# Channel group 1 of a long convolution goes through its products as stationary operand instead of a turn through DRAM, with strided PSUM evictions, q in long rows and a new written order

## The chip, the cores and the metric

The kernel runs on one core of one Trainium2 chip. The metric is device time in microseconds (us): 199.32 us is the median of three timed runs of the kernel before (198.66 to 200.85). A separate execution was recorded by the hardware profiler. The engines are TensorE (PE, matmuls and, beside them, its weight loads, PEld), VectorE (DVE), ScalarE (ACT), GpSimd (POOL) and SyncE (SP), which here issues every DMA. SBUF is the memory that the engines work in, PSUM the small memory that PE writes to and that DVE and ACT empty ("evict").

## The reference

Two independent computations on 2048 positions and 576 channels, in bf16, whose results stand side by side in the output (2048 x 1152).

```python
# A: a gated long convolution
k_shift = sum(k_pad[:, t:t+S, :] * shift_k[:, 3 - t] for t in range(4))   # 4 taps along the positions
kv = k_shift * v
y = causal_convolution(kv, ssm_k)      # length 2048 per channel, by FFT of 4096
y = y + kv * ssm_D
a = q * y
# B: linear attention, 32 heads of 18 channels
q, k, v = split(x @ wqkv)
phi = lambda t: where(t > 0, t + 1, exp(t)) + 1e-6
kv = phi(k)^T v ; z = sum(phi(k))      # per head
o = (phi(q) kv) / (phi(q) z + 1e-6)
b = o @ wo
out = concat([a, b], -1)
```

## The kernel before

**Part A.** A position n is written as 16 a + b, with a on the 128 partitions. The convolution is a product of two transforms of 128 x 16 frequencies.

- `conv_piece`: the four taps on DVE or POOL, per piece of 128 channels (`HP`, the last has 64) and half of b: `tap` (L427, products), `tap+` (L432) and `tapx` (L435, sums), `tapv` (L438, product with v).
- `h_piece` and `s1`: PE transposes the filter (L465), `hD` (L477) adds ssm_D into its first row, and `s1` (L515) does the 128-point transform with the table `Gsb` as stationary operand. Its result is evicted into C (`Ch` of the filter, `Cu` of the signal).
- `s2`: DVE transposes 32x32 blocks (L532, `ct`), PE does the 16-point transform in 32x32 tiles (L541), and the result goes into `su`. For the filter pieces in `HDMA` a transposing DMA (L490, `cq`) and a full-width matmul (`s2q`, L498) take the place of these, with an eviction `s2evq` into `TT`. The evictions are made by the helper `copy`: ACT at L259, DVE at L261.
- `inv`: per block of 64 channels, two DMAs swap neighbouring rows of TT (`X`), two products with su are formed on DVE or POOL (L562, `p0` and `p1`), and the inverse 16-point transform follows.
- Its result has to be turned so that the 128 frequencies lie on partitions. Channel groups (`QG`): 0 and 1 have 256 channels, 2 has 64. For the groups in `DR` PE works in 32x32 tiles (`i1`, L572), the result is evicted into U, written to DRAM (`Vw`, tensor `v_scr`) and read back turned as V (`Vr`). For the others the products are the stationary operand (`i1s`, L591), so that the matmul's result is turned already; it is evicted into V directly (`i1evs`), and `i2` reads V with a stride.
- `inv2`: the 128-point inverse transform with the table `Esb` (`i2`, L627 and L630), the product with q (`i2q`, L637), and the store (`yo`).

**Part B.** `kproj` (L660 matmul, L663 exp, L666 the rest of phi) and `qproj` (L678, L682, L686, L689) need x with channels on partitions. Two of the four x tiles are transposed by PE (L336), two by transposing DMAs (L348, L351). `b_G` (L716) forms x^T phi(k), from which `M` (L826) follows; `dmm` gives the denominators, their reciprocal is spread by `b_bc` (L843) and multiplied in (`pqn`, `pqg`). `b_out` (L877) is the output projection, a row block in two halves of five matmuls, with evictions `oev` into ob and a store `oo`.

**What sets the order.** Every operation is registered with `P.op`. The string `PLAN` lists all of them in one written order with the engine that does each (P, A, D, G for POOL, S for SP); an engine takes its own in that order, and so does SP's DMA queue. `PLACES` gives each buffer its address and PSUM bank. `FILL` puts filler matmuls of no use (L927) ahead of some operations. `PORT` names the DVE and POOL operations that work on SBUF alone: one of POOL's is made to wait for the last of DVE's that stands before it in the order.

Of the kernel before, what the change touches and what calls it, by code (L numbers as in the profile page):

```python
# [26 lines left out]
DR = (0, 1)  # L27
# [191 lines left out]
def kernel(  # L219
# [226 lines left out]
    def h_piece(pc):  # L446
# [27 lines left out]
        def hd(e):  # L474
            d = Drow.t[0:1, c0:c0 + n]
            o = hT.t[0:1, 0, :]
            nc.vector.tensor_tensor(  # L477
# [5 lines left out]
        for g in range(n // PCH):  # L483
            sp = SB("TT", [128, 2, 8, 128, 2])
            TX[c0 // PCH + g] = sp
            if not dt:
# [5 lines left out]
                rd=[C], wr=[cq], name="trq", tx=_dma(524288, 256), bias=(nm, 0.0))  # L492
            for hh in range(2):
                ps = psb(2, "s2ps")

                def mm(e, hh=hh, ps=ps, cq=cq):
# [5 lines left out]
                    e, sp.t[:, 0, 4 * hh:4 * hh + 4].rearrange("p w k t -> p w t k"),  # L502
                    ps.t.rearrange("p b (w t k) -> p (b w) t k", w=2, t=2)),
# [51 lines left out]
    def inv(g, su, bias):  # L555
# [28 lines left out]
        for hh in range(2):  # L584
# [10 lines left out]
            def ev(e, hh=hh, ps=ps):  # L595
                o0 = c0 + 32 * hh
                copy(e, V[vg].t[:, :, o0:o0 + 32].rearrange("p r (q j) -> p q r j", j=4),
                     ps.t.rearrange("p b c -> p (b c)").rearrange("p (q r j) -> p q r j", q=8, j=4))
            P.op(either(1024), ev, rd=[ps], wr=[(V[vg], (g, hh))], name="i1evs", bias=bias)

    def inv2(vg, bias):
        c0, n = QG[vg]
        qb = SB("q%d" % vg, [128, 16, n], side=1)
        load("qA", qb, lambda e: dma(qb.t[:], ap(q, c0, [[16 * D, 128], [D, 16], [1, n]])), 4096 * n, row=2 * n,
             bias=(bias[0], -5.0))
        nb = 512 // n
        if vg in DR:
            dtok = P.buf("vd%d" % vg, [128, 1], space="dram")
            for kh in range(4):
                load("Vw", None, lambda e, kh=kh: dma(  # L610
                    ap(V_d[vg], 32 * n * kh, [[128 * n, 32], [1, 32 * n]]),
                    U[vg].t[32 * kh:32 * kh + 32].rearrange("p k c -> p (k c)")), 2048 * n, rd=[U[vg]],
# [5 lines left out]
        for bg in range(16 // nb):  # L618
            ps = psb(1, "i2ps")

            def mm(e, bg=bg, ps=ps):
                for j in range(nb):
                    b = nb * bg + j
                    for ri in range(2):
                        v_ = V[vg].t[:, 2 * b + ri, :]
                        if vg in DR:
                            nc.tensor.matmul(ps.t[:, 0, n * j:n * j + n], lhsT=Esb.t[:, b, ri, :], rhs=v_,  # L627
                                             start=(ri == 0), stop=(ri == 1))
                            continue
                        nc.tensor.matmul(ps.t[:, 0, n * j:n * j + n], lhsT=Esb.t[:, b, ri, :],  # L630
                                         rhs=bass.AP(tensor=v_.tensor, offset=v_.offset,
                                                     ap=[list(v_.ap[0]), [64, n // 64], [1, 4], [4, 16]]),
                                         start=(ri == 0), stop=(ri == 1))

            def mul(e, bg=bg, ps=ps):
                qs = qb.t[:, nb * bg:nb * bg + nb, :]
# [390 lines left out]
```

## Time and profile before

| | before |
|---|---|
| median of three timed runs | 199.32 us |
| profiled execution, its own time | 196.29 us |
| span, first to last instruction | 194.5 us |
| PE busy | 163.6 us (84%), of which fillers at L927 15.4 us |
| DVE busy | 152.1 us (78%) |
| ACT busy | 123.1 us (63%) |
| POOL busy | 86.1 us (44%) |
| mean granted PE clock | 0.957 |
| moved by DMA | 40.52 MB, 208 GB/s in the mean |

An engine's busy time counts its instructions only, not its waits. Matmuls are pipelined, so a busy PE is not PE at its peak. The page's second part cuts the span into 40 slices, one digit each for the busy tenths. The chain of waits goes back from the last instruction, at each step to what released it; "SPq" in it is SP's queue issuing a DMA, "issue" is time without a visible wait. A group row gives line, engine, operation, what it writes and reads with shapes, the count, then busy us and mean ns of one, then the idle time ahead of the group and what ended it.

### The profile page before, as it was taken

The page shows a single profiled execution, that of the slowest core. Times are in us where ns is not written, and L with a number is a line of the kernel's source. Part 1 is how long each engine was busy: PE and PEld are TensorE (multiplying, and loading weights), DVE is VectorE, ACT ScalarE, POOL GpSimd, SP SyncE. Part 2 cuts the span into 40 slices and gives each one's busy share as a digit, 9 for nine tenths or more (in the row PEclk, how much of TensorE's full clock was granted, in tenths as well). Part 3 has the DMA queues.
Part 4 walks back from the last instruction along what each step waited for, and adds up shares of the span by engine and source line. Part 5 has one row for each costly group of instructions (what it writes and reads, how often), then busy time and mean ns, then how long its engine had stood idle before and what let it go on. Part 6 is the DMA issues. An engine that isn't in the chain of part 4 may idle for free.

```text
span 194.5 us, 4394 instructions
## 1 busy us (share of the span) xinstructions
PE 163.6 (84%) x1803; PEld 113.9 (59%) x1812; DVE 152.1 (78%) x182; ACT 123.1 (63%) x174; POOL 86.1 (44%) x47
## 2 busy tenths in 40 slices
PE   7597889989469999999999877779899947998580
PEld 5296657547347756777777454337356626887360
DVE  0019998998978999999989997799999849544370
ACT  2366857666638875425379999999999925424000
POOL 8002367380480081604189999599650250800000
PEclk9759999999969999999999999999999999999697
DMA  5999999898970346590289996424059699999996
GB/s 136 360 380 259 377 243 201 218 275 275 193 222 0 105 98 135 115 357 21 81 228 266 249 181 205 165 108 166 4 108 278 194 276 318 217 266 272 311 264 207
DMA packets 51264, 40.52 MB, mean 208 GB/s; under 512 B 25323, under 2 KB 48108, under 8 KB 50348
## 3 DMA queue, kind: packets, MB, share of 16 engines
q1 hardware_dynamic: 51244, 40.24, 77.7%
q8 instruction: 14, 0.23, 0.5%
q14 instruction: 6, 0.05, 0.1%
HBM read 21.62 MB, written 8.91 MB: 157 GB/s over the span
## 4 chain that ended last, share of the span: by engine, by line
DVE 28%; DMA 27%; PE 19%; ACT 11%; SPq 7%; issue 5%; DVEq 0%; ACTq 0%
DMA wq<-in_B_wqkv_dram 8%; DMA V<-v_scr 7%; DVE m L427 6%; SPq L251 6%; DMA wk<-in_B_wqkv_dram 4%; ACT TT L259 4%; DMA v<-in_A_v_dram 4%; DMA v_scr<-U 4%; PE ps_all L877 4%; PE ps_all L660 3%; DVE hT L477 3%; PE ps_all L678 3%; DVE ct L532 2%; DVE U L261 2%; DVE pqT L689 2%
## 5 line engine op out<-in xcount | busy, mean ns | idle before, releaser
L562 POOL TENSOR_TENSOR TT<-su,TT 128x2048 bf16<-128x2048 bf16 x8 | 32.4, 4070 | 12.4 <-ACT su L259 9.4
L660 PE MATMUL ps_all<-wk,xT 128*128 128x288 bf16 x160 | 22.9, 286 | 3.8 <-DMA xT<-in_B_x_dram 3.3
L432 POOL TENSOR_TENSOR m<-m 128x2048 bf16<-128x2048 bf16 (+1 forms) x4 | 14.3, 3577 | 22.0 <-DVE m L427 14.9
L515 PEld LDWEIGHTS <-Gsb 128*128 128x128 bf16 x320 | 19.2, 102 | 6.0 <-issue 3.5
L660 PEld LDWEIGHTS <-xT 128*128 128x128 bf16 x160 | 15.2, 98 | 10.1 <-DMA xT<-in_B_x_dram 3.6
L427 DVE TENSOR_TENSOR m<-kb,Wj 128x4096 bf16<-128x4096 bf16 (+1 forms) x10 | 20.6, 2071 | 0.0
L663 ACT ACTIVATE ek<-ps_all,neg 128x288 bf16<-128x288 f32 x32 | 15.8, 500 | 7.6 <-PE ps_all L660 6.6
L716 PE MATMUL ps_all<-pk,x_sb 128*128 128x289 bf16 (+1 forms) x160 | 20.6, 287 | 0.0
L678 PE MATMUL ps_all<-xT,wq 128*128 128x512 bf16 x75 | 19.5, 392 | 1.3 <-DMA wq<-in_B_wqkv_dram 0.9
L877 PE MATMUL ps_all<-M,pqT 128*128 128x288 bf16 x128 | 20.0, 286 | 0.0
L637 DVE TENSOR_TENSOR q<-ps_all,q 128x512 bf16<-128x512 f32 x18 | 11.8, 686 | 10.1 <-PE ps_all L627 7.5
L927 PE MATMUL ps_all<-fz 128*128 128x256 bf16 x87 | 15.4, 303 | 5.0 <-DVE fz L906 1.1
L716 PEld LDWEIGHTS <-x_sb 128*128 128x128 bf16 x160 | 15.3, 98 | 4.2 <-issue 0.2
L686 ACT ACTIVATE eq<-ps_all,neg 128x512 bf16<-128x512 f32 x18 | 12.4, 689 | 7.7 <-PE ps_all L678 6.9
L259 ACT ACTIVATE TT<-ps_all 128x1024 bf16<-128x1024 f32 x13 | 16.6, 1307 | 0.3 <-PE ps_all L541 0.3
L666 DVE SCALAR_TENSOR_TENSOR pk<-ek,ps_all 128x288 bf16<-128x288 bf16 x32 | 13.4, 445 | 3.3 <-ACT ek L663 3.3
L259 ACT ACTIVATE Cu<-ps_all 128x1024 bf16<-128x1024 f32 (+1 forms) x16 | 15.3, 1026 | 0.0
L435 POOL TENSOR_TENSOR m<-m 128x1024 bf16<-128x1024 bf16 x4 | 8.5, 2128 | 15.0 <-DVE m L432 15.0
L259 ACT ACTIVATE su<-ps_all 128x1024 bf16<-128x1024 f32 x12 | 12.0, 1060 | 4.9 <-PE ps_all L541 4.9
L627 PE MATMUL ps_all<-V,Esb 128*128 128x256 bf16 x64 | 9.6, 299 | 6.4 <-DMA V<-v_scr 6.4
L438 POOL TENSOR_TENSOR v<-m,v 128x1024 bf16<-128x1024 bf16 (+1 forms) x6 | 11.9, 1977 | 6.4 <-DVE m L427 6.2
L877 PEld LDWEIGHTS <-pqT 128*128 128x128 bf16 x128 | 12.1, 98 | 4.2 <-issue 1.3
(105 smaller groups left out, 328.1 us busy)
## 6 DMA issues: line engine op xcount, KB each, us to landing
TT<-TT SPq DMA_DIRECT2D x18, 256.0 KB, 3.2
v_scr<-U SPq DMA_DIRECT2D x8, 512.0 KB, 6.4
V<-v_scr SPq DMA_DIRECT2D x8, 512.0 KB, 6.4
x_sb<-in_B_x_dram SPq DMA_DIRECT2D x4, 576.0 KB, 7.7
kb<-in_A_k_dram SPq DMA_DIRECT2D x2, 1152.0 KB, 13.6
v<-in_A_v_dram SPq DMA_DIRECT2D x2, 1152.0 KB, 13.3
out_dram<-ob SPq DMA_DIRECT2D x16, 144.0 KB, 4.3
q<-in_A_q_dram SPq DMA_DIRECT2D x2, 1024.0 KB
```

What stands on the lines that cost most here:

```text
L259: nc.scalar.activation(out=o, in_=i, func=ACTF.Copy)
L427: return nc.vector.tensor_tensor(out=m.t[:], in0=i0, in1=i1, op=ALU.mult)
L432: lambda e: tt(e)(out=m.t[:, 0:2], in0=m.t[:, 0:2], in1=m.t[:, 2:4], op=ALU.add),
L515: nc.tensor.matmul(pf[:, n * j:n * j + n], lhsT=Gsb.t[:, 8 * bg + j, ri, :], rhs=src(8 * bg + j), start=True, stop=True)
L562: P.op({"DVE": _dve(2048, 2), "POOL": _pool(2048)}, lambda e, x=x: tt(e)(out=tx.t[:, x], in0=su.t[:], in1=tx.t[:, x], op=ALU.mult), rd=[su ...
L660: nc.tensor.matmul(ps.t[:, 0, 0:HALF], lhsT=xT.t[:, t, 128 * (r % 4):128 * (r % 4) + 128], rhs=wk.t[:, t, HALF * hh:HALF * hh + HALF], sta ...
L663: P.op(("ACT", _act(HALF) + 0.085), lambda e, hh=hh, ps=ps: nc.scalar.activation(out=eb.t[:, hh], in_=ps.t[:, 0, 0:HALF], func=ACTF.Exp, b ...
L666: P.op(("DVE", _dve(HALF)), lambda e, hh=hh, ps=ps: nc.vector.scalar_tensor_tensor(out=pk.t[:, r, HALF * hh:HALF * hh + HALF], in0=eb.t[:, ...
L678: nc.tensor.matmul(ps.t[:, 0, :], lhsT=wq.t[:, t, 128 * c:128 * c + 128], rhs=xTg[g].t[:, t, :], start=(t == 0), stop=(t == 4))
L716: nc.tensor.matmul(ps.t[:, 0, 0:n], lhsT=x_sb.t[:, r, FT[t]:FT[t] + 128], rhs=pk.t[:, r, HALF * hh:HALF * hh + n], start=(r == 0), stop=(r ...
L877: nc.tensor.matmul(ps.t[:, 0, 0:HALF], lhsT=pqT.t[:, c, 128 * r:128 * r + 128] if c < 4 else pqt.t[:, 128 * (r % 8):128 * (r % 8) + 128], ...
L927: nc.tensor.matmul(b.t[:, 0, 0:256], lhsT=fz.t[:, 0:128], rhs=fz.t[:], start=True, stop=True)
```

## The change

`DR` holds group 0 alone, so group 1 takes the way of group 2. `i1evs` writes V in the natural order of channels and reads PSUM with a stride for it; `i2` then reads V without one, in all groups. `s2evq` reads PSUM with a stride and writes SBUF in one run, where it read in one run and wrote every other element. q is one buffer for all channels, loaded in two DMAs with rows of 9216 bytes instead of three with rows of 512 and 128; the products with q and the stores work on slices of it. `hD` joins `PORT`. The planner's prices of two kinds of DMA (`tx`) are changed. `FILL`, `PLAN` and `PLACES` are new: the order, the choice of DVE, ACT or POOL for operations that several can do, and all addresses. The fillers go from 87 to 31.

```diff
-DR = (0, 1)
+DR = (0,)
...
         def hd(e):
...
-            nc.vector.tensor_tensor(
+            return nc.vector.tensor_tensor(
...
                 P.op(either(1024), lambda e, hh=hh, ps=ps, sp=sp: copy(
-                    e, sp.t[:, 0, 4 * hh:4 * hh + 4].rearrange("p w k t -> p w t k"),
-                    ps.t.rearrange("p b (w t k) -> p (b w) t k", w=2, t=2)),
+                    e, sp.t[:, 0, 4 * hh:4 * hh + 4],
+                    ps.t.rearrange("p b (w t k) -> p (b w) k t", w=2, t=2)),
                     rd=[ps], wr=[(sp, hh)], name="s2evq", bias=(nm, 0.0))
...
             def ev(e, hh=hh, ps=ps):
-                o0 = c0 + 32 * hh
-                copy(e, V[vg].t[:, :, o0:o0 + 32].rearrange("p r (q j) -> p q r j", j=4),
-                     ps.t.rearrange("p b c -> p (b c)").rearrange("p (q r j) -> p q r j", q=8, j=4))
+                copy(e, V[vg].t[:, :, c0:c0 + 64].rearrange("p r (j q) -> p r j q", j=4)[:, :, :, 8 * hh:8 * hh + 8],
+                     ps.t.rearrange("p b c -> p (b c)").rearrange("p (q r j) -> p r j q", q=8, j=4))
             P.op(either(1024), ev, rd=[ps], wr=[(V[vg], (g, hh))], name="i1evs", bias=bias)
+
+    qb = SB("q", [128, 16, D], side=1)
+    for hh in range(2):
+        load("qA", qb, lambda e, hh=hh: dma(qb.t[:, 8 * hh:8 * hh + 8, :], ap(
+            q, 8 * hh * D, [[16 * D, 128], [D, 8], [1, D]])), 1179648, wr=[(qb, hh)], row=9216)
...
-        qb = SB("q%d" % vg, [128, 16, n], side=1)
-        load("qA", qb, lambda e: dma(qb.t[:], ap(q, c0, [[16 * D, 128], [D, 16], [1, n]])), 4096 * n, row=2 * n,
-             bias=(bias[0], -5.0))
...
                     for ri in range(2):
-                        v_ = V[vg].t[:, 2 * b + ri, :]
-                        if vg in DR:
-                            nc.tensor.matmul(ps.t[:, 0, n * j:n * j + n], lhsT=Esb.t[:, b, ri, :], rhs=v_,
-                                             start=(ri == 0), stop=(ri == 1))
-                            continue
                         nc.tensor.matmul(ps.t[:, 0, n * j:n * j + n], lhsT=Esb.t[:, b, ri, :],
-                                         rhs=bass.AP(tensor=v_.tensor, offset=v_.offset,
-                                                     ap=[list(v_.ap[0]), [64, n // 64], [1, 4], [4, 16]]),
-                                         start=(ri == 0), stop=(ri == 1))
+                                         rhs=V[vg].t[:, 2 * b + ri, :], start=(ri == 0), stop=(ri == 1))
...
             def mul(e, bg=bg, ps=ps):
-                qs = qb.t[:, nb * bg:nb * bg + nb, :]
+                qs = qb.t[:, nb * bg:nb * bg + nb, c0:c0 + n]
...
-PORT = ("tap", "tap+", "tapx", "tapv", "p0", "p1", "pqg", "pqe")
+PORT = ("tap", "tap+", "tapx", "tapv", "p0", "p1", "pqg", "pqe", "hD")
...
 FILL = """
-9:23 416:4 22:10 114:7 96:1 120:2 491:1 292:1 296:2 588:1 584:2 309:2 499:1 602:2 648:1 549:3 538:2 579:2 591:2 621:3
-346:1 709:1 702:4 711:9
+9:17 11:1 414:5 26:4 33:2 544:2
 """
```

What the new order does on each engine, by the names above:

- SP: the loads of x come before those of k, and both halves of v behind wq and two x tiles. The four writes `Vw` of group 0 stand behind the last two evictions into U; then come seven stores `oo`, then the four reads `Vr`.
- PE: all but one block of `kproj` and all of `qproj` stand ahead of the filter pieces 1 to 4. 17 of the 32 halves of `b_out` stand ahead of the last `i1`, 15 behind it. Group 1's `i1s` and `i2` come ahead of most of group 0's `i2`.
- DVE: behind the last eviction into U stand nine products, one `su`, one `i1evs`, three `oev` and the 18 products with q. ACT: five `su`, nine `i1evs`, 13 `oev`.
- POOL: eight of the products before become six, the last `p1` of block 4; 12 are DVE's.

More of the change, by code (lines that the diff above doesn't have):

```diff
@@ L645, in inv2 @@
                     ap(outd, b4 * 2 * D + c0, [[16 * 2 * D, 128], [2 * D, YB], [1, n]]),
-                    qb.t[:, b4:b4 + YB, :]), 256 * YB * n,
-                     rd=[(qb, k) for k in range(b4 // nb, (b4 + YB) // nb)], wr=[], bias=bias, row=2 * n)
+                    qb.t[:, b4:b4 + YB, c0:c0 + n]), 256 * YB * n,
+                     rd=[(qb, (vg, k)) for k in range(b4 // nb, (b4 + YB) // nb)], wr=[], bias=bias, row=2 * n)
     P.op(("POOL", 0.3), lambda e: nc.gpsimd.memset(pk.t[:, :, D:D + 1], EPS), wr=[(pk, "e")], name="pke", bias=500)
```

67 lines of the change are left out of this document (33 added, 34 removed), and 27 rows, old and new, of the table PLACES.

## The prediction

> **What bounds the kernel now.** I read the page first: its busy times, and its rows of forty slices of 4.86 us.
>
> ```profile
> span 194.5 us, 4394 instructions
> ...
> PE 163.6 (84%) x1803; PEld 113.9 (59%) x1812; DVE 152.1 (78%) x182; ACT 123.1 (63%) x174; POOL 86.1 (44%) x47
> ...
> PE   7597889989469999999999877779899947998580
> ...
> DVE  0019998998978999999989997799999849544370
> ...
> PEclk9759999999969999999999999999999999999697
> ...
> GB/s 136 360 380 259 377 243 201 218 275 275 193 222 0 105 98 135 115 357 21 81 228 266 249 181 205 165 108 166 4 108 278 194 276 318 217 266 272 311 264 207
> ```
>
> VectorE (DVE) is at nine tenths or more in most slices between the fourth and the thirty-first, and falls to 3 to 5 tenths near the end. No engine is full all the time, so the next view is the busy time by stretch. I cut at 20.4 us (first convolution tap), 78.5 (last feature map of q), 143.2 (last eviction into U of channel group 0) and at the end; one more cut looks into the middle.
>
> ```profile
> 0.00:20.40 20.40, 16.10 (x141) 12.55 (x142) 6.83 (x9) 9.87 (x11) 5.20 (x15) 0.83 0.93 289
> 20.40:78.50 58.10, 51.55 (x425) 34.55 (x429) 53.25 (x73) 40.11 (x65) 25.89 (x13) 0.97 0.79 192
> 78.50:143.20 64.70, 57.24 (x762) 38.19 (x764) 61.09 (x65) 51.59 (x63) 46.12 (x17) 1.00 0.59 159
> 143.20:194.50 51.30, 38.73 (x481) 28.58 (x479) 30.94 (x41) 21.52 (x38) 8.93 (x4) 0.94 0.96 257
> ...
> 96.00:156.00 60.00, 52.42 (x809) 32.90 (x811) 56.05 (x57) 58.25 (x73) 43.66 (x15) 1.00 0.69 181
> ```
>
> After each time come the busy us of PE, weight loads, DVE, ACT and POOL. Up to 143.2 us DVE works 6.83 + 53.25 + 61.09 = 121.2 us and loses 22.0, of which 13.6 lie before the first tap. From 96 to 156 us ACT is busy 58.25 of 60 us and DVE 56.05: there the evictions of both engines bound. In the last 51.3 us DVE works 30.9 and ACT 21.5: here a wait bounds. The chain of waits names it (start, us, what):
>
> ```profile
> 12.36 15.52 DMA wq<-in_B_wqkv_dram
> ...
> 51.78 3.77 DVE hT L477
> ...
> 142.02 1.22 DVE U L261
> ...
> 146.16 7.76 DMA v_scr<-U
> ...
> 156.40 8.07 DMA V<-v_scr
> ...
> 164.51 1.03 PE ps_all L627 x8
> 165.54 6.74 PE ps_all L877 x55
> 172.28 1.84 PE ps_all L591 x32
> ...
> 174.86 1.03 ACT V L259
> ...
> 176.82 5.17 DMA V<-v_scr
> ...
> 182.04 1.86 PE ps_all L627 x8
> ...
> 188.73 0.69 DVE q L637
> 189.42 0.59 DVEq L1022
> ```
>
> The last U eviction of group 0 ends at 142.02 + 1.22 = 143.2. Then U goes to DRAM (7.76 us), comes back as V (8.07), and the same turn for group 1 ends with another 5.17 us of return. The stationary-product way, which group 2 takes already, costs 1.84 us of PE and a 1.03 us eviction in this chain. Early, the load of wq holds PE to 12.36 + 15.52 = 27.88 us.
>
> **The change part by part.** The durations are group means (busy us, mean ns):
>
> ```profile
> L259 ACT ACTIVATE TT<-ps_all 128x1024 bf16<-128x1024 f32 x13 | 16.6, 1307 | 0.3 <-PE ps_all L541 0.3
> ...
> L927 PE MATMUL ps_all<-fz 128*128 128x256 bf16 x87 | 15.4, 303 | 5.0 <-DVE fz L906 1.1 <-ACT TT L259 1.1 <-ACT U L259 0.5
> ...
> L259 ACT ACTIVATE Cu<-ps_all 128x1024 bf16<-128x1024 f32 x12 | 12.8, 1116 | 0.0
> ...
> L259 ACT ACTIVATE su<-ps_all 128x1024 bf16<-128x1024 f32 x12 | 12.0, 1060 | 4.9 <-PE ps_all L541 4.9
> L562 DVE TENSOR_TENSOR TT<-su,TT 128x2048 bf16<-128x2048 bf16 x10 | 11.8, 1206 | 0.0
> L637 DVE TENSOR_TENSOR q<-ps_all,q 128x512 bf16<-128x512 f32 x18 | 11.8, 686 | 10.1 <-PE ps_all L627 7.5 <-PE ps_all L630 2.5
> ...
> L261 DVE CAST su<-ps_all 128x1024 bf16<-128x1024 f32 x6 | 7.2, 1208 | 0.6 <-ACT GT L728 0.6
> ...
> L477 DVE TENSOR_TENSOR hT<-hT,Drow 1x128 bf16<-1x128 bf16 x4 | 6.3, 1566 | 0.4 <-ACT hT L259 0.4
> ...
> L261 DVE CAST ob<-ps_all 128x288 bf16<-128x288 f32 x8 | 3.5, 452 | 2.6 <-PE ps_all L877 1.6 <-ACT ob L259 1.0
> ...
> L630 PE MATMUL ps_all<-V,Esb 128*128 128x64 bf16 x32 | 2.2, 235 | 0.3 <-ACT ob L259 0.3
> ...
> L259 ACT ACTIVATE V<-ps_all 128x1024 bf16<-128x1024 f32 x1 | 1.0, 1025 | 2.1 <-PE ps_all L877 2.1
> ```
>
> *The stretch after the last U eviction (now 51.3 us).* The written order of the changed kernel leaves these behind that eviction.
> DVE: nine products (9 x 1.206), one su (1.208), one V eviction (taken like su), three ob (3 x 0.452) and the 18 products with q (18 x 0.686): 10.9 + 1.2 + 1.2 + 1.4 + 12.3 = 27.0 us.
> ACT: five su (5.3), nine V evictions (9 x 1.025 = 9.2) and 13 ob (taken like DVE's: 5.9): 20.4 us.
> PE: 15 half rows of the output projection, five matmuls each at 6.74 / 55 = 0.123 us (9.2 us); ten halves of the stationary step at 1.84 / 2 = 0.92 (9.2); 18 groups of the last transform, 16 of four matmuls at 1.03 / 8 = 0.129 (8.3) and two of group 2 (2.2 us by L630); three groups of 16 small matmuls (half a stationary half each as an estimate, 1.4): 30 us. Before, PE had 32 half rows there, four block steps of 32x32 tiles and two stationary halves.
> All three would fit into 30 us; what joins them is this. The last product of groups 1 and 2 ends about 12.5 us after the U eviction (nine products, one su, one ob). One stationary half and its eviction on ACT follow (0.92 + 1.03), so the first transform of group 1 starts at about +14.5. Then the 18 products with q follow each other (12.3 us): +27. Two ob on DVE (0.9) come next; the issue of the last stores and their landing take what lies behind the last product today, 194.5 - 189.42 = 5.1 us. That is +33; for waits of one engine for another on the way I add 2: **35 us** (bounds: 30, PE's own sum, and 41, with twice the waits and a late landing). 51.3 - 35 = 16.3 us less.
> The DRAM turn of group 0 stays. It takes from 143.2 to 164.5 = 21.3 us until the last part of V is used; its products now come after those of group 1, from about +19 to +26, so the work of group 1 hides it, with little to spare.
>
> *Up to the last U eviction (now 143.2 us).*
> (a) Among the loads, half of v moves from ahead of wq to behind it, and x comes before k:
>
> ```profile
> v<-in_A_v_dram SPq DMA_DIRECT2D x2, 1152.0 KB, 13.3
> ```
>
> At the 259 to 377 GB/s of the page's slices 2 to 5, 1152 KB less bring wq in 3 to 4.5 us earlier. The first tap needs kb, which now stands behind 576 KB more of x and lands a little later, but DVE has x to work on meanwhile. I take **-2.5** (0 to -4.5).
> (b) The addition of D to the first row of hT (L477) is 1x128 elements and yet takes 1.566 us in the mean, 3.77 us of the chain in one place. There it ends at 51.78 + 3.77 = 55.55, just behind this POOL operation:
>
> ```profile
> 51.26 4.05 POOL L432 TENSOR_TENSOR m<-m 128x2048 bf16<-128x2048 bf16 x1 [7.63 <-DVE m L427]
> ```
>
>  The change counts it among the operations that are kept apart from POOL's. Four such at 1.57 instead of about 0.3: **-4** (0 to -5).
> (c) DVE gets more to do ahead of this point: nine ob (4.1 us), eight copies of M, xT and hT (some 0.7 each, between ob and su by size: 5.6), and eight operations of the size of su (four Cu, one of them half, two ct, one bb, one product: 9.1); four Ch, four su and four TT leave it, less one half Ch (13.9). 18.8 - 13.9 = 4.9, of which I leave 0.9 to the overlap of neighbours: **+4** (2 to 5).
> (d) PE gets 17 half rows of the output projection, 17 x 5 x 0.123 = 10.4 us, and loses most of its filler matmuls (L927), 87 before and 31 by the new list. PE is busy 51.55 + 57.24 of 122.8 us there, so part shows: **+3** (0 to +10.4).
> (e) ACT makes all 14 TT evictions of the second transform instead of 11. They now read PSUM with a stride of 512 bytes and write in one run; before they read in one run and write every other element, and take 1.307 us in the mean against 1.060 for su, the same size in one run both ways (the 13 hold two of that kind; the 11 others come to (13 x 1.307 - 2 x 1.06) / 11 = 1.35). No row shows a strided read. From below the su row bounds it, from above nothing in this trace does; I use 1.06, the row of the same size and output, which makes 14 x 1.06 = 14.8 instead of 11 x 1.35 = 14.9: **0**. The group 1 evictions into V read with such a stride as well and I keep their 1.025. Twice these, 2.1, is the upper end that I price as a rival.
> (f) q in two long loads instead of three of short rows: they lie beside work and are wanted only at +15: 0. If they came late, the products with q would wait for them; the bytes are the same.
> 143.2 - 2.5 - 4 + 4 + 3 = 143.7.
>
> *The sum.* 143.7 + 35 = 178.7 us of span. The profiled execution took 196.29 us with a span of 194.5, so 180.5 by its own time; the median of the runs, 199.32, lies 3.0 above that execution. I forecast **183 us**, 8% faster. A measurement of this kernel can tell about 1% from no change.
>
> **The rivals.**
> *Strided reads of PSUM (slower than before).* 23 of the 24 evictions that now read PSUM with a 512-byte stride are ACT's. If one took 2.1 us, twice the 1.03 to 1.06 of a run, the 14 in the middle would add 14 x 0.75 = 10 us over today's 1.35, where ACT has 1.75 us of idle time in 60, and nine V evictions would add 9 x 1.05 = 9.5 ahead of the last transform. 183 + 10 + 9.5 is 202 to 203. It decides from about 1.9 us per eviction. Against it: ACT's groups of 1024 elements lie between 1.025 and 1.35 whatever the pattern of their writes, Cu with short runs at 1.116. For it: no row shows such a read. Chance 0.10.
> [...]
>
> *The DRAM turn of group 0 takes the place of that of group 1.* SP issues seven stores of output rows between the four writes and the four reads, four before; the reads wait in SP's queue behind them and those for their evictions. If the turn grows from 21.3 to 30 us, the last two groups of V, their products, store and landing (0.9 + 1.4 + 5.1) end at +38.5 instead of +35: 187. Against it: less else is in the DMA queues then. Chance 0.12.
>
> *A starved first half.* Two of the x tiles come as transposing loads behind wq. Before, one such wait cost PE 3.26 us, and the clock after it:
>
> ```profile
> 54.20 0.79 PE L660 MATMUL ps_all<-wk,xT 128*128 128x288 bf16 x5 [3.26 <-DMA xT<-in_B_x_dram]
> 55.59 1.03 PE L515 MATMUL ps_all<-hT,Gsb 128*128 128x128 bf16 x8 [0.61 <-DVE hT L477]
> ...
> 59.14 0.61 PE L515 MATMUL ps_all<-hT,Gsb 128*128 128x128 bf16 x8
> ```
>
> Eight matmuls of L515 take 1.03 us after it, and 0.61 once that is over. Two such waits (2 x 3.3), a loss of 2 behind them, and the head's gain gone (2.5) give 183 + 11 = 194. Chance 0.10.
> [...]
>
> *PE becomes the bound*: all 10.4 us of (d) show and no cover is left; 183 + 7.4 = 190. Chance 0.08. That the change does not do what it says can be left out for group 1: its writes to DRAM and reads are gone from the order.
>
> **How the numbers follow.** The forecast has 0.60. The lowest sum of the bounds is 143.2 - 4.5 - 5 + 4 + 30 = 167.7, or 172.5 by the runs' median; it needs every gain at once, so the range begins at 175. The three faster rivals reach 187 to 194. So 175 to 194, which leaves out the strided reads (0.10) and some of each end. Faster by over 1%: all but the strided reads and the worst of the starved half, 0.86; within 1%: 0.04; slower: 0.10.
>
> **What would show it.** In the profile after: no V<-v_scr return later than about 165 us; the last U eviction near 144; a stretch behind it of some 35 us in which DVE is busy over 27; L477 below 0.5 us in the mean; TT evictions on ACT near 1.06, and V evictions near 1.03; wq landed by 24 us. Wrong it would be by TT and V evictions of 1.5 us or more, by PE waiting for xT or for V over 3 us at a time, or by a last U eviction behind 150 us.

## The result, and the profile after

The changed kernel takes **172.16 us** in the median (172.02 to 172.78, four runs) beside 198.99 us (196.62 to 200.85, four runs) of the kernel before on the same chip. The ratio is **0.869, 95% interval 0.861 to 0.877**. The forecast of 183 us (175 to 194) had the sign right and is 10.8 us too slow; the time lies 2.8 us below its range. Executions over 1.5% above the fastest of their kernel, here the one of 200.85 us, are left out of the ratios; medians are from all.

The page of the changed kernel, with its span, busy times and slices (now 4.26 us each):

```profile
span 170.3 us, 4267 instructions
...
PE 157.6 (93%) x1746; PEld 113.1 (66%) x1756; DVE 143.4 (84%) x189; ACT 120.2 (71%) x171; POOL 74.7 (44%) x43
...
PE   7999999999999999999999798989999999964992
...
DVE  0138999999988999979998999999999998783761
...
PEclk9999999999999999999999999999999999998799
```

PE is at nine tenths or more almost throughout, and its granted clock, which before fell to 0.50 in three places (8 to 14, 56 to 58 and 182 to 184 us), is 1.00 up to 156 us (then 0.57 to 158 us and 0.50 to 159). The same by stretch, cut at the changed kernel's own last eviction into U, which ends at 133.9 us (columns as in the prediction):

```profile
0.00:20.40 20.40, 19.01 (x168) 14.37 (x169) 9.05 (x13) 11.61 (x14) 5.20 (x15) 1.00 0.93 283
20.40:78.50 58.10, 57.89 (x500) 40.04 (x503) 55.13 (x85) 40.34 (x69) 24.52 (x13) 1.00 0.64 176
78.50:133.90 55.40, 51.80 (x715) 35.29 (x720) 54.08 (x62) 50.76 (x64) 45.00 (x15) 1.00 0.78 214
133.90:170.30 36.40, 28.88 (x369) 23.44 (x367) 25.13 (x33) 17.51 (x27) 0.00 (x0) 0.95 0.88 232
```

Up to the last U eviction, PE's idle time falls from 4.3 + 6.6 + 7.5 = 18.3 us (the three stretches before, in the prediction) to 1.4 + 0.2 + 3.6 = **5.2 us**, while its busy time rises from 124.9 to 128.7. DVE's busy time falls from 121.2 to 118.3 and what it loses from 22.0 to 15.6. The stretch behind shrinks from 51.3 to **36.4 us**, for which 35 was forecast.

PE's waits from 20 us to the last U eviction, the two longest before and then the two longest after (us in total, times, longest):

```profile
PE ps_all L660 <- DMA xT<-in_B_x_dram: 3.3, 1, 3.3
PE ps_all L927 <- ACT TT L259: 1.1, 2, 0.5
```

```profile
PE ps_all L837 <- DVE pqT L851: 0.7, 1, 0.7
PE ps_all L837 <- DVE Cu L261: 0.4, 1, 0.4
```

No load stops PE in this stretch any more. The groups that the prediction named:

```profile
L259 ACT ACTIVATE TT<-ps_all 128x1024 bf16<-128x1024 f32 x17 | 17.1, 1039 | 0.9 <-PE ps_all L541 0.6 <-PE ps_all L498 0.3
L921 PE MATMUL ps_all<-fz 128*128 128x256 bf16 x31 | 6.9, 382 | 1.2 <-DVE fz L900 1.1 <-DVE Cu L261 0.2
L259 ACT ACTIVATE V<-ps_all 128x1024 bf16<-128x1024 f32 x9 | 8.8, 1070 | 3.2 <-PE ps_all L591 2.8 <-DMA out_dram<-ob 0.3
L477 DVE TENSOR_TENSOR hT<-hT,Drow 1x128 bf16<-1x128 bf16 x4 | 1.3, 327 | 1.3 <-ACT hT L259 1.2
L261 DVE CAST V<-ps_all 128x1024 bf16<-128x1024 f32 x1 | 1.2, 1224 | 0.2 <-PE ps_all L591 0.2
```

The TT evictions take 1.04 us, like those into su (1.04), which read in one run: there the strided read of PSUM shows no cost. Those into V take 1.07 on ACT and 1.22 on DVE, beside 1.02 and 1.22 in e_turn (below), where they read in one run. L477 is at 0.33 us. The end of the chain of waits (start, us, what):

```profile
129.78 2.94 DMA out_dram<-ob
132.72 0.52 DVE U L261
...
143.40 3.90 PE ps_all L591 x63
...
147.39 0.38 SPq L251
147.77 0.04 issue
147.81 7.58 DMA V<-v_scr
155.39 0.04 issue
155.44 4.47 PE ps_all L626 x24
...
163.66 3.24 PE ps_all L871 x25
166.90 0.02 issue
166.92 0.41 ACT ob L259
```

One DRAM turn is left in it, that of group 0, whose reads are issued at 147.39 us, behind seven stores. Ahead of this, the chain lies on PE from 20.25 to 84.83 us and then mostly on POOL, which has no share in the chain of the kernel before:

```profile
85.67 4.07 POOL m L432
...
106.48 4.08 POOL TT L562
...
112.64 4.03 POOL TT L562
...
118.73 8.12 POOL TT L562 x2
```

From 85.67 to 126.84 us POOL is busy 40.9 of 41.2 us, ACT 40.2, DVE 40.0 and PE 37.9. So no one engine can be named as the bound there, and no run below changes POOL's work.

### The profile page after: what moved, and what is told of

The parts are those of the page before. It is cut to its first block, busy times and chain, and to the rows that moved or that the text cites. A ratio compares the mean times of both kernels' runs of the same rounds, so it can differ in the third digit from the quotient of the medians.

```text
span 170.3 us, 4267 instructions
## 1 busy us (share of the span) xinstructions
PE 157.6 (93%) x1746; PEld 113.1 (66%) x1756; DVE 143.4 (84%) x189; ACT 120.2 (71%) x171; POOL 74.7 (44%) x43
## 4 chain that ended last, share of the span: by engine, by line
PE 52%; POOL 21%; DVE 11%; DMA 6%; issue 6%; SPq 2%; ACT 0%; POOLq 0%; DVEq 0%
POOL TT L562 11%; PE ps_all L672 10%; PE ps_all L654 10%; PE ps_all L710 9%; PE ps_all L515 5%; DMA V<-v_scr 4%; POOL pqT L847 4%; DVE TT L562 4%; PE ps_all L921 3%; PE ps_all L465 3%; PE ps_all L626 3%; POOL m L432 2%; PE ps_all L591 2%; PE ps_all L871 2%; SPq L251 2%
## 5 line engine op out<-in xcount | busy, mean ns | idle before, releaser
L562 POOL TENSOR_TENSOR TT<-su,TT 128x2048 bf16<-128x2048 bf16 x6 | 24.4, 4074 | 2.7 <-DVE ob L261 2.7
L654 PE MATMUL ps_all<-wk,xT 128*128 128x288 bf16 x160 | 21.6, 286 | 0.1
L710 PE MATMUL ps_all<-pk,x_sb 128*128 128x288 bf16 (+1 forms) x160 | 21.2, 286 | 0.0
L871 PE MATMUL ps_all<-M,pqT 128*128 128x288 bf16 x128 | 20.4, 287 | 0.7 <-DVE U L261 0.3
L432 POOL TENSOR_TENSOR m<-m 128x2048 bf16<-128x2048 bf16 (+1 forms) x4 | 14.3, 3582 | 12.8 <-DVE dcol L801 8.5
L438 POOL TENSOR_TENSOR v<-m,v 128x1024 bf16<-128x1024 bf16 x5 | 10.6, 2129 | 20.3 <-DVE v L438 10.8
L259 ACT ACTIVATE Ch<-ps_all 128x1024 bf16<-128x1024 f32 (+1 forms) x16 | 15.3, 973 | 5.5 <-PE ps_all L515 5.3
L672 PE MATMUL ps_all<-xT,wq 128*128 128x512 bf16 x76 | 18.0, 379 | 0.2
L259 ACT ACTIVATE ob<-ps_all 128x288 bf16<-128x288 f32 x20 | 7.7, 425 | 13.4 <-PE ps_all L871 13.4
L259 ACT ACTIVATE su<-ps_all 128x1024 bf16<-128x1024 f32 x16 | 15.8, 1042 | 1.2 <-PE ps_all L541 1.2
L562 DVE TENSOR_TENSOR TT<-su,TT 128x2048 bf16<-128x2048 bf16 x12 | 14.5, 1248 | 0.4 <-ACT su L259 0.4
L660 DVE SCALAR_TENSOR_TENSOR pk<-ek,ps_all 128x288 bf16<-128x288 bf16 x32 | 13.1, 448 | 1.6 <-ACT ek L657 1.6
L626 PE MATMUL ps_all<-V,Esb 128*128 128x256 bf16 (+1 forms) x96 | 10.1, 271 | 3.6 <-DMA V<-v_scr 3.6
```

The lines of the kernel that those rows point to most:

```text
L259: nc.scalar.activation(out=o, in_=i, func=ACTF.Copy)
L432: lambda e: tt(e)(out=m.t[:, 0:2], in0=m.t[:, 0:2], in1=m.t[:, 2:4], op=ALU.add),
L562: P.op({"DVE": _dve(2048, 2), "POOL": _pool(2048)}, lambda e, x=x: tt(e)(out=tx.t[:, x], in0=su.t[:], in1=tx.t[:, x], op=ALU.mult), rd=[su ...
L654: nc.tensor.matmul(ps.t[:, 0, 0:HALF], lhsT=xT.t[:, t, 128 * (r % 4):128 * (r % 4) + 128], rhs=wk.t[:, t, HALF * hh:HALF * hh + HALF], sta ...
L660: P.op(("DVE", _dve(HALF)), lambda e, hh=hh, ps=ps: nc.vector.scalar_tensor_tensor(out=pk.t[:, r, HALF * hh:HALF * hh + HALF], in0=eb.t[:, ...
L672: nc.tensor.matmul(ps.t[:, 0, :], lhsT=wq.t[:, t, 128 * c:128 * c + 128], rhs=xTg[g].t[:, t, :], start=(t == 0), stop=(t == 4))
```

## The experiments

U is the end of the last eviction into U of group 0 in the trace of the run (143.2 before, 133.9 after). A dash stands where no time was read from the trace.

| run | what | median, us | ratio to before (95%) | U, us |
|---|---|---|---|---|
| after | the changed kernel | 172.16 | 0.869 (0.861 to 0.877) | 133.9 |
| e_turn | old order, group 1 without DRAM | 190.00 | 0.969 (0.957 to 0.982) | 142.1 |
| e_stride | old order, strided TT evictions | 196.53 | 0.999 (0.994 to 1.004) | 142.4 |
| e_hd | old order, hD in PORT | 197.60 | 1.007 (1.001 to 1.013) | 142.7 |
| e_code | old order, these three | 189.22 | 0.963 (0.952 to 0.973) | 141.7 |
| e_hd2 | old order, hD freed of POOL | 197.25 | 0.994 (0.989 to 1.000) | 142.3 |
| e_load | old order, v behind wq | 198.63 | 1.003 (0.996 to 1.009) | 141.4 |
| e_fill | old order, 17 fillers in the head | 198.74 | 0.993 (0.987 to 1.000) | - |
| e_pe10 | old order, 96 fillers in the middle | 204.78 | 1.028 (1.016 to 1.039) | - |
| e_xt | old order, last xT load earlier | 202.48 | 1.018 (1.005 to 1.031) | 147.4 |
| e_xt_hd | e_xt and e_hd2 | 195.79 | 0.989 (0.984 to 0.995) | 141.1 |
| e_code_hl | e_code, e_hd2 and e_load | 187.90 | 0.953 (0.943 to 0.962) | 139.3 |
| a_load | new order, v ahead of wq | 173.64 | 0.877 (0.870 to 0.884) | 137.1 |
| a_oldstride | new order, old TT evictions | 174.94 | 0.880 (0.872 to 0.888) | 136.6 |
| a_pe10 | new order, 98 fillers to 63 us | 181.58 | 0.918 (0.911 to 0.926) | 145.4 |
| a_pe10b | new order, 96 fillers behind | 176.88 | 0.896 (0.886 to 0.905) | 140.1 |
| a_dve4 | new order, 4 us more of DVE | 174.34 | 0.874 (0.862 to 0.886) | - |
| a_vr | new order, reads of V earlier | 172.04 | 0.870 (0.864 to 0.875) | 134.4 |
| a_best | a_vr and output rows earlier | 181.28 | 0.919 (0.910 to 0.927) | 134.4 |

**The edits parted from the order.** My theory was that the order carries what the forecast missed; the rival, that the edits do. Each edit went into the kernel before in its old order. For e_turn the entries of `PLAN` and `PLACES` were carried over one by one (`i1` became two `i1s`, V of group 1 took the place of U, `Vw` and `Vr` of group 1 went).

```diff
 e_turn
-DR = (0, 1)
+DR = (0,)
...
 e_stride
-                    e, sp.t[:, 0, 4 * hh:4 * hh + 4].rearrange("p w k t -> p w t k"),
-                    ps.t.rearrange("p b (w t k) -> p (b w) t k", w=2, t=2)),
+                    e, sp.t[:, 0, 4 * hh:4 * hh + 4],
+                    ps.t.rearrange("p b (w t k) -> p (b w) k t", w=2, t=2)),
...
 e_hd
-PORT = ("tap", "tap+", "tapx", "tapv", "p0", "p1", "pqg", "pqe")
+PORT = ("tap", "tap+", "tapx", "tapv", "p0", "p1", "pqg", "pqe", "hD")
```

> The kernel before in its own order; only channel group 1 takes the stationary products (each block step becomes its two stationary halves at the same place, the four writes to DRAM and four reads of that group are gone). In the profile before, the return of group 1 ends at 181.99 us and eight products with q come behind it. Theory (the order carries most of the change): the products of group 1 follow those of group 2 at once, some 6 to 7 us earlier, time 192 to 194 us; the last U eviction stays near 143. Rival (the DRAM turn is nearly all of it): 178 or less.

> The kernel before in its own order; only the 14 TT evictions of the second transform read PSUM with a 512-byte stride and write in one run. By the changed kernel's groups one takes 1.04 us in place of 1.35 on ACT. Theory (order carries most): 11 x 0.3 = 3.4 us less of ACT, of which 0 to 3 show: 196 to 199 us. Rival (ACT's evictions bound the middle and give the missed 10 us): 189 or less.

> The kernel before in its own order; only the addition of D (hD, L477) is kept apart from POOL's operations: the next POOL operation of the listed kinds waits for it. Theory: L477 falls from 1.57 us to 0.3 in the mean and the time by 2 to 5 us, 194 to 197. Rival (POOL starts later instead, nothing gained): 198 to 200.

> The three edits above together in the order of the kernel before (q still in three loads of short rows). This parts the edits from the order searched anew. Theory (the order carries the miss): 186 to 190 us, the last U eviction at 137 to 140 and not at the 133.9 of the changed kernel. Rival (the edits carry all of it, and the new order little): 172 to 177, with the last U eviction near 134.

e_turn came out at 0.969, 190.00 us where 192 to 194 were expected, by the stretch behind U, which is 188.4 - 142.1 = 46.3 us in place of 51.3. e_stride did not move the time, as expected; e_hd missed its theory (194 to 197) and stands 0.7% above the kernel before. Their groups, first e_stride, then e_hd:

```profile
L259 ACT ACTIVATE TT<-ps_all 128x1024 bf16<-128x1024 f32 x13 | 13.2, 1030 | 0.0
```

```profile
L477 DVE TENSOR_TENSOR hT<-hT,Drow 1x128 bf16<-1x128 bf16 x4 | 6.3, 1567 | 0.4 <-ACT hT L259 0.4
```

The cheaper eviction is there, 1.03 in place of 1.31 us, and saves 3.4 us of ACT that the old order does not need. L477 is as slow as before: POOL's operation stands ahead of hD in the written order, so making POOL wait for hD changes nothing. These three edits together (e_code) give 0.963, 7.4 us, with U at 141.7. The rest, 188.0 - 170.3 = 17.7 us by the spans, comes with the new order, that is with its fillers, its choice of engines and q's long loads as well. Of these, 141.7 - 133.9 = 7.8 lie ahead of U and 46.3 - 36.4 = 9.9 behind it. The rival is out. e_code's time is in the theory's range; its U, at 141.7, is later than the 137 to 140 expected, so the edits gave less ahead of U than the theory itself allowed them.

**PE's price.** Term (d) of the prediction let 3 us show of PE's additional work. Fillers were added ahead of the k projection (a_pe10), between the projections and the last U eviction in the new order (a_pe10b) and there in the old order (e_pe10); for a_pe10, `FILL` gets 3 or 4 at each of 28 groups of k, and the other two have 96 spread likewise:

```diff
 FILL = """
-9:17 11:1 414:5 26:4 33:2 544:2
+9:17 11:1 414:5 26:4 33:2 544:2 107:3 137:4 149:3 116:4 146:3 152:4 101:3 98:4 209:3 227:4 134:3 140:4 224:3 173:4
+170:3 143:4 185:3 191:4 206:3 176:4 188:3 155:4 182:3 221:4 218:3 215:4 179:3 212:4
```

> The changed kernel with 98 more filler matmuls (128x256, some 0.11 us each, about 10 us of PE) ahead of the last 28 groups of the k projection; nothing else differs. It prices PE work in the first part, where PE is busy 57.89 of 58.1 us. Theory 1 (PE's busy time there is partly waiting that the records count, DVE bounds): 172 to 176 us. Theory 2 (PE bounds the first part now): 180 to 183.

> The changed kernel with 96 more filler matmuls (some 10 us of PE) spread over the groups from the last projection to the last U eviction, 63 to 134 us, where the 17 half rows of the output now stand. In the first part such fillers cost 9.4 us. Theory 1 (DVE and ACT bound there, PE has some 4 us of idle time): 4 to 7 us more, 176 to 179. Theory 2 (PE bounds there as well, its work shows in full): 180 to 182. Term (d) as forecast was 3 of 10.4: 175.

> The kernel before with 96 more filler matmuls (10 us of PE) spread over the groups between the last projection and the last U eviction. It answers term (d), what 10.4 us more of PE work costs in that stretch, in which PE was busy 57.24 of 64.7 us. Term (d) as forecast: 3 us more (0 to 10.4), 200 to 202 us. Rival (DVE and ACT bound there and PE's extra work is free): 197 to 199.

a_pe10, the rows that answer to those of the changed kernel:

```profile
20.40:78.50 58.10, 58.10 (x480) 41.09 (x478) 45.56 (x73) 34.20 (x59) 22.36 (x12) 1.00 0.63 170
78.50:145.40 66.90, 63.70 (x851) 44.46 (x850) 64.68 (x75) 58.43 (x76) 47.13 (x16) 1.00 0.66 186
145.40:179.90 34.50, 27.36 (x369) 22.47 (x366) 25.09 (x32) 17.46 (x27) 0.00 (x0) 1.00 0.94 245
```

PE's busy time over the span is 10.0 us above that of the changed kernel, the time 9.4: theory 2 holds, **PE bounds the changed kernel to 63 us**, and DVE falls from 55.13 to 45.56 busy us of the same 58.1. Behind that, 96 fillers (9.8 us by the same price) cost 4.7 us and move U by 6.2, in theory 1's range. The 6.2 are the 9.8 less the 3.6 us that PE idled from 78.5 us to U; with the fillers PE is busy 61.09 of the 61.6 us there. In the old order they cost 2.8% (1.6 to 3.9), 5.5 us; my rival, that PE's work is free there, is out.

The other side, DVE's price: nine `kphi` twice, the same values written again.

```diff
             got = o.fn(o.eng)
+            if o.id in (229, 136, 226, 145, 187, 193, 157, 223, 190):
+                got = o.fn(o.eng)
```

> The changed kernel with nine of the kphi operations of the k projection done twice on DVE (9 x 0.45 = 4.0 us of DVE work, the same values written again). By the run with more PE work there PE bounds the first part. Theory (PE alone bounds to 63 us, DVE has 2.9 us of idle time in 20 to 78): 0 to 1.5 us more, 172 to 173.7. Rival (DVE bounds as well): 4 us more, 176.

Ratio 0.874 beside 0.869: 1 us, within both intervals. 4 us of DVE work do not show as 4; whether they show at all, these runs do not tell.

**Single causes, taken from the new order.** One half of v went ahead of wq again (the head of SP's entries), and the TT evictions got their old patterns (the edit of e_stride the other way round).

```diff
-S15 S45 S14 S16 S44 S49 S50 S42 S47 S430 S46 S431 S17 S43
+S15 S45 S14 S16 S17 S44 S49 S50 S42 S47 S430 S46 S431 S43
```

> The changed kernel; one half of v is loaded ahead of the larger part of wq again, as in the kernel before. It prices the load order alone. Theory of the prediction (term (a)): wq lands 3 to 4.5 us later and the time rises by 2 to 4.5 us, 174 to 177. Rival (the head is bound by x and the first tap, wq has room): within 1 us of 172.

> The changed kernel with the access patterns that the kernel before has for the TT evictions of the second transform: PSUM read in one run, every other element written. They go from 1.04 to 1.35 us on ACT, 14 times, 4.3 us. Theory (DVE bounds, ACT has some idle time in the middle): 172 to 174.5 us. Rival (ACT's evictions bound and the cheaper form is what the forecast missed): 176 or more.

a_load, PE's longest wait from 14 to 66 us, and a_oldstride's group:

```profile
PE ps_all L672 <- DMA wq<-in_B_wqkv_dram: 2.6, 1, 2.6
```

```profile
L259 ACT ACTIVATE TT<-ps_all 128x1024 bf16<-128x1024 f32 x17 | 22.2, 1357 | 0.7 <-PE ps_all L541 0.6
```

With v ahead PE waits 2.6 us for wq, and U comes 3.2 us later; 1.5 us of it are left at the end (0.877, between the two expectations). The old patterns cost 0.32 us more in the mean of this group, three of whose 17 evictions are of another kind, so some 0.39 for each of the 14 (an estimate); U comes 2.7 us later, the time is 2.8 us longer, a little above the theory's range. Both intervals overlap with that of the changed kernel. So in the new order both edits are worth some 3 us ahead of U, each by one trace, and in the old one, by e_stride and by e_load below, 0.8 and 1.8 there.

**Single causes, repaired in the old order.** hD of h1 went ahead of a tap on DVE and POOL's `tapv` behind hD of h2, beside the edit of e_hd (e_hd2); half of v went behind wq (e_load); the first group of fillers grew (e_fill).

```diff
 e_hd2, DVE's entries, then POOL's G90 against DVE's
-D170 D79 D197 D434 D182
+D170 D434 D79 D197 D182
-D530 G90 D459
+D530 D459 G90
...
 e_load, SP's entries
-S45 S19 S17 S44 S274
+S45 S19 S44 S17 S274
...
 e_fill
-9:23
+9:40
```

> The kernel before, with the two long additions of D freed of their POOL neighbours: hD of h1 one tap earlier on DVE, and POOL's tapv of conv7 behind hD of h2; hD counted among the kept-apart operations. The run that only counted it (first study) left L477 at 1.57 us, since the POOL operation was ahead of it in the order. Theory (term (b)): L477 at 0.2 to 0.4 us, 3.5 + 1.5 us less on DVE, time 193 to 195. Rival (DVE waits elsewhere for the same time): 197 to 199.

> The kernel before, with the half of v that stands ahead of wq in SP's queue behind it instead; nothing else. Theory (term (a)): wq lands some 3 us earlier than 27.88 us, time 194 to 196 us. Rival (PE and DVE have other work till then): 197 to 199.

> The kernel before with 17 more filler matmuls in the first group (40 in place of 23), to close the 2 us of idle PE between 4.9 and 8.2 us, behind which the granted clock is half until 14.1 us. Theory (the half clock in the head delays what follows): granted clock 1.00 in the first 20 us, time 1 to 3 us lower, 195 to 197. Rival (the loads bound the head): 197 to 199 with a full clock.

The group of e_hd2:

```profile
L477 DVE TENSOR_TENSOR hT<-hT,Drow 1x64 bf16<-1x64 bf16 x1 | 1.9, 1850 | 0.0
L477 DVE TENSOR_TENSOR hT<-hT,Drow 1x128 bf16<-1x128 bf16 x4 | 1.3, 317 | 0.6 <-ACT hT L259 0.6
```

The time, 0.994, is on the rival's side. L477 falls from 6.5 us in all to 3.1; one stall moved on to the next hD (h4, 1.85 us; the POOL operation that had been put off stands ahead of it in the written order). U comes 0.9 us earlier, the time falls by 0.6%.

In e_load the first matmul with wq starts at 26.1 us in place of 28.1, and U comes 1.8 us earlier. What is left of it at the end stays open: the ratio is 1.003, but the ten executions spread from 194.13 to 200.04 us, three of them below the 197.57 that the kernel before took beside them in the median. The first 20 us of e_fill:

```profile
0.00:10.00 10.00, 8.95 (x48) 5.82 (x49) 0.17 (x1) 2.23 (x2) 4.17 (x13) 1.00 0.79 262
10.00:20.00 10.00, 8.34 (x127) 6.89 (x126) 7.14 (x8) 7.80 (x10) 1.04 (x2) 1.00 1.08 338
```

The granted clock is 1.00 in both halves, and the time 0.7% lower (0 to 1.3): the half clock in the head was a small cost, at the low end of the 1 to 3 us expected. Three causes that I had priced at 1 to 5 us each give less than 1% each by their ratios.

One reason could be that two waits lie beside each other: before, PE waits for xT to 54.20 us, while hD holds DVE to 55.54. So the last xT load was moved ahead, alone and with e_hd2.

```diff
-S534 S50 S21 S47 S275 S478 S429 S43 S716 S535 S545 S49 S20
+S534 S50 S49 S21 S47 S275 S478 S429 S43 S716 S535 S545 S20
```

> The kernel before, with the transposing load of the last x tile (xT, issued at 48.66 us) moved ahead in SP's queue to 35 us. In the kernel before PE waits for it 3.26 us, to 54.20, while DVE is held by hD to 55.54. Theory (two waits beside each other, one hides the other): little alone, the last U eviction 142 to 143.2, time within 1% of before. Rival (PE's wait alone carries the loss between 50 and 60 us): U at 139 to 140, 3 to 4 us faster.

> The kernel before with both: the last x tile loaded earlier, and the two long additions of D freed of their POOL neighbours as in e_hd2. Theory (the two waits have to go together): the last U eviction at 138.5 to 140.5, time 193 to 195. Rival (neither wait matters, PE and DVE sums bound): U at 142 or later, time within 1% of before.

Neither expectation holds for e_xt: it is slower, U at 147.4. PE's longest waits from 20 us to 143 in it:

```profile
PE ps_all L660 <- POOL xT L354: 4.5, 1, 4.5
PE ps_all L515 <- DVE hT L477: 3.2, 1, 3.2
```

The load that I moved went past another, the tail of the tile before it (`xTt`, S47), which was issued at 40.33 in place of 36.89 us; POOL's memset of that tile ended at 45.50 in place of 41.55, and PE waited for it, and later for hD. With hD freed (e_xt_hd) U is at 141.1 and the time 1.1% lower, between the two expectations, and PE still waits 3.0 us for that memset. That the two waits hide each other is consistent with 147.4 against 141.1, a step of 6.3 us from hD, which gave 0.9 by itself; it isn't shown cleanly, since my move made a wait of its own.

Last, the repairs that helped, with the three edits:

> The old order with the three edits (as e_code), and with the two repairs that helped: half of v behind wq, and the two long additions of D freed of POOL. Theory (small repairs add, the rest of the gain is the order as a whole): the last U eviction at 138.5 to 139.5, time 185 to 187.5. Rival (named causes suffice once they are together): U at 136 or earlier, 183 or less. Third (they hide one another): U at 141 or later, 188 or more.

U at 139.3, time 187.9, 0.953: by U as the theory had it, by the time 0.4 us above its range. The repairs add 2.4 us to the edits ahead of U; **5.4 us to the changed kernel's 133.9 belong to the order as a whole** (with q's loads and the fillers in it), and these runs do not part them further. One stretch of 10 us shows where some of them lie, first in e_code_hl and then in the changed kernel:

```profile
50.00:60.00 10.00, 7.47 (x54) 4.96 (x53) 5.40 (x11) 6.44 (x12) 6.21 (x3) 0.83 0.66 158
```

```profile
50.00:60.00 10.00, 9.95 (x94) 6.78 (x94) 9.04 (x14) 7.19 (x12) 6.44 (x3) 1.00 0.27 78
```

PE is busy 7.47 us of it and DVE 5.40 in the one, 9.95 and 9.04 in the other. In e_code_hl PE still waits 2.3 us for a transposing load of x and 1.6 us for POOL's memset behind another, its two longest waits ahead of U; the changed kernel issues the last of these loads at 28.2 us, the kernel before at 48.7, and the changed kernel has neither wait.

**The DRAM turn of group 0, and a try to go on.** In the changed kernel PE waits 3.57 us for V. In a_vr the four reads stand ahead of five of the seven stores.

```diff
-S669 S362 S372 S332 S402 S347 S382 S387 S674 S675 S673 S672 S352
+S669 S362 S372 S674 S675 S673 S672 S332 S402 S347 S382 S387 S352
```

> The changed kernel; in SP's queue the four reads of V of group 0 (Vr) stand behind two of the seven stores of output rows instead of behind all seven. In the changed kernel they were issued at 147.39 to 149.95 us, 4.5 us and more after the last write had landed (142.94), and DVE waits 3.32 + 0.94 + 0.33 us for the products that need them. Theory (the turn of group 0 is back on the path, through the order of SP's queue): reads issued near 143, landed near 152, time 168 to 170 us. Rival (DVE's sum of work sets the end, or the five stores behind cost as much): 171.5 to 173.

The rival was right. The chain says why the reads gained so little:

```profile
137.24 9.23 DMA v_scr<-U
...
146.56 0.38 SPq L251
```

They go out at 146.56 us, 0.8 earlier than in the changed kernel and not near 143, because the last write lands at 146.47; the 142.94 of the expectation was the landing of another write. So the seven stores held the reads by about 1 us only. The last product with q ends 2.6 us earlier (161.57 for 164.21), the last landing comes 0.7 us earlier (168.4 for 169.1), and the time is the same. The stores put off come back at the end. a_best therefore moved work as well: the reads ahead of all seven stores, and the last seven half rows of the output, with their evictions (all on ACT) and stores, ahead of group 0's `i2`, where PE waits; one output buffer and two PSUM banks got other places for it. SP's entries, then PE's:

```diff
-S669 S362 S372 S332 S402 S347 S382 S387 S674 S675 S673 S672 S352 S702 S711 S693 S717 S714 S684 S337 S407 S357 S377
+S669 S674 S675 S673 S672 S372 S362 S332 S402 S347 S382 S387 S352 S337 S357 S407 S377 S702 S711 S693 S717 S714 S684
...
-P666 P691 P709 P689 P685 P682 P687 P676 P715 P712 P678 P333 P680 P355 P405 P335 P375 P353 P373
+P666 P333 P335 P355 P353 P405 P375 P373 P691 P709 P689 P685 P682 P687 P676 P715 P712 P678 P680
```

> The changed kernel with two moves in the tail: the four reads of V stand directly behind the four writes in SP's queue, ahead of all seven stores; and the last seven half rows of the output with their evictions (all on ACT) and stores stand ahead of the products of group 0, where PE waits 3.57 us for V. Theory (the end is now the last product with q and its store): last product near 161.5 to 162.5, end 3 us behind it at 165.5, time 168 to 170. Rival (the stores' transfers fill the DMA queues in the tail, share 0.88, and set the end): 171 to 173.

181.28 us, 9 us slower. The timeline of ACT and then of PE in its tail:

```profile
156.99 1.02 ACT L259 ACTIVATE V<-ps_all 128x1024 bf16<-128x1024 f32 x1 [9.07 <-DMA out_dram<-ob]
...
158.06 2.72 PE L626 MATMUL ps_all<-V,Esb 128*128 128x256 bf16 x12 [7.92 <-ACT V L259]
```

ACT waits 9.07 us for a store to land before it can evict into V of group 2: that V lies where a buffer of output rows was, and the store that frees it now stands behind the reads. In the changed kernel that store goes out ahead of the reads, and ACT waits 0.33 us there. No run was measurably faster than the changed kernel.

## Why the prediction was right or wrong

**The sum.** The forecast was 143.7 to U + 35 behind it + 1.8 + 3.0, 183.5 before rounding. Seen were 133.9 + 36.4 + 1.75 (172.05 for the profiled execution) + 0.1. So 9.8 us of the miss lie ahead of U and 2.9 in the last term: the changed kernel's median does not stand 3 us above its profiled execution. The tail took 1.4 more than forecast. The range could not hold this: its lowest sum, 167.7, has (c) at +4 and not at that term's own lower bound of +2, which gives 165.7, 170.5 by the runs' median.

**The stretch behind U was right.** Its size, 36.4 for 35, and its parts: DVE busy 25.1 us for my sum of 27.0 and PE 28.9 for 30. One joint in it failed: the first product with q starts at +14.5 as forecast, but the last one ends at +30.3 and not at +27, since DVE waits 3.32 + 0.94 + 0.33 us where the products need V of group 0, whose turn I took for hidden. The smaller sum of DVE and the 2 us allowed for waits made up for most of it, which is partly luck. The runs add what the gain is made of: taking group 1 out of DRAM gives 5 of its 15 us, the new order the other 10, which includes the 17 half rows of output that moved ahead.

**Up to U the failing step is (d).** By DVE's account, with the windows of both kernels: the head (to 20.4 us) loses 2.2 us less, against **-2.5** in (a); L477 takes 5.0 less, against **-4** in (b); other work of DVE rises by 2.1, against **+4** in (c); and DVE's losses behind the head fall from 8.5 to 4.3, **-4.2**, where (d) had put +3 for PE's work showing. These are -9.3 for my +0.5. (d) carries 7.2 of the 9.8, (c) 1.9.

The price in (d) was not too high: PE's work shows by half in the middle (4.7 us for 9.8 in a_pe10b, 5.5 in e_pe10) and nearly in full ahead of it (9.4 for 10.0 in a_pe10). What failed is its account of PE. Up to U PE's busy time rose by only 3.8 us: 13.6 of output rows came, but the fillers fell from 12.8 to 6.9, and the same matmuls of the k and q projections took 39.7 us in place of 42.4, in a stretch whose granted clock is 1.00 in place of 0.97. And 13.1 us of idle time went, for which the sum had no term: 143.2 + 3.8 - 13.1 = 133.9. I had asked what each named edit does to the waits of the kernel before, and left all waits that no edit names as they stood. The new order removed many of them. Both accounts are sums that come out for any cause; that the order did it and not the named edits is what e_code and e_code_hl show, and which of its moves did it stays open.

**(a) and (b) as causes.** The account agrees with (a), and so do a_load (3.2 us) and e_load (1.8), by U. The reading that wq holds PE to 27.88 us was too strong: before, PE waits 0.9 us for it. For (b) the stall is gone as said, but not by the reason that I gave: `PORT` does nothing for it in the old order (e_hd, 1.567 us in the mean); the new order puts four of the five hD where no POOL operation runs (0.21 to 0.36 us), and the fifth, at 91.94 us, takes 0.37 us although POOL's L273 runs beside it. Freeing two of them in the old order (e_hd2) brought U 0.9 us earlier. **(e)** holds: 1.04 us for a forecast 1.06. **(f)** was not tried alone.

**The rivals.** *Strided reads of PSUM*: out, the TT evictions took 1.03 to 1.04 us in four kernels (e_stride, e_code, a_load and the changed one), and those into V 1.07 on ACT and 1.22 on DVE; the rival was to decide from about 1.9. *A starved first half*: out, no load stops PE from 20 us to the last U eviction. *The DRAM turn of group 0*: half seen. To the landing of its third read it grew from 19.6 us (143.2 to 162.8) to 23.3 (133.9 to 157.2), and PE waits 3.57 us for it, over the 3 that I had named as a sign of being wrong; but reads that went out 0.8 us earlier (a_vr) did not move the end. Its price was also added up wrongly: 30 + 0.9 + 1.4 + 5.1 is 37.4 and not 38.5, so 185 and not 187. *PE the bound*: right as a statement up to 63 us (a_pe10), wrong as a price, since PE could be the bound only because its idle time was gone.

## What to carry to other kernels

Where a whole order is searched anew, add up the busy time and the idle time of the busiest engines, and ask which of the idle time still has a reason in the new order; a sum over the named edits leaves every other wait where it was. Before, PE and DVE idled 18 and 22 us up to the same point, and the gain up to there came out of that room: 13.1 and 6.4 us of it. Single repairs in a written order are poor measures of a cause: three gave under 1% each, and two moves of a load or a store past others cost 4 and 9 us, because what they passed fed a memset or freed a buffer. And a time of landing is worth checking against the last transfer of its group: one such misreading carried an expectation here (a_vr).

## What the runs showed of the hardware

ACT's TT evictions of 128x1024, which read PSUM with a 512-byte stride (two of 13 and three of 17 of them are of the plain form), took 1.03 to 1.04 us in the mean in four kernels, and those into su, read in one run, 1.04 in the changed kernel. The group with the form that reads in one run and writes every other 2-byte element takes 1.31 us in the mean in the kernel before and 1.357 in a_oldstride, with as many of the plain form in it.

In the kernel before, two additions of 1x128 elements on DVE (L477) took 3.84 us (from 51.70, beside POOL's L432 of 51.26 to 55.31) and 1.84 us (from 79.61, beside POOL's L438 of 79.08 to 81.21), and each ended 0.23 to 0.24 us behind the POOL operation; one with no POOL operation beside it took 0.37 (from 65.36). One of 1x64 elements took 1.85 us in e_hd2, and 0.25 in the changed kernel (from 84.67, no POOL operation beside it). Not every addition beside a POOL operation took so long: in the changed kernel an addition of 1x128 took 0.37 us at 91.94, in the middle of POOL's L273, which adds a constant to a tensor in SBUF from 89.82 to 92.59.

In e_fill the granted clock is 1.00 in both halves of the first 20 us, where the kernel before has 0.50 from 8 to 14 us, and the time is 0.7% lower (0 to 1.3).
